# The front of a fused attention and MLP kernel: first batch's q, k loaded in FP32, two blocks' distances added by matmul, second pair ahead of the first layer

## Chip, core and metric

The kernel runs on one core of a Trainium2 chip. The metric is the device time of one launch in microseconds (us); the kernel before has a median of 307.6 us over three runs (307.52 to 308.02). The profile names the engines PE (TensorE), DVE (VectorE), ACT (ScalarE), POOL (GpSimd) and SP (SyncE).

## What is computed

Attention with a sliding window of 128 keys and a linear penalty on distance (ALiBi), for 8 batches, 8 heads, 576 tokens and 64 elements a head; then, on the 512 values of each token, a layer norm with a gain, two weight matrices with a ReLU between them, and a residual.

```python
scores = scale * np.matmul(q, k.transpose(0, 1, 3, 2))
slopes = 2.0 ** (-8.0 * (np.arange(H, dtype=np.float32) + 1) / H)
bias = slopes[:, None, None] * (-np.abs(rel).astype(np.float32))[None, :, :]
mask = (rel >= 0) & (rel < window)
scores = np.where(mask, scores + bias[None], -1000000000.0)
...
attn = np.exp(scores)
attn = attn / (np.sum(attn, axis=-1, keepdims=True) + 1e-09)
return np.matmul(attn, v).astype(np.float32)
...
xn = (x - mu) / np.sqrt(var + 1e-06) * g_ln
ch = np.maximum(xn @ w_ch1, 0.0) @ w_ch2
return (x + ch).astype(np.float32)
```

Inputs and output are FP32 in HBM; the kernel computes in FP16 with FP32 sums.

## The kernel before

**Blocks and groups.** Batches are taken in pairs. A pair has nine blocks of 128 rows: blocks 0 to 7 alternate between the two batches (block 2i is rows 128i of the first batch, block 2i+1 the same rows of the second), block 8 holds the last 64 rows of both. `order` lists the 36 blocks. The MLP takes them in groups: four groups of two blocks, then seven of four (`GROUPS`). Groups 0 and 1 are blocks 0 to 3 of the first pair.

**What one block goes through.** `turn` transposes q and k of two blocks (one of each batch) on PE, 64 matmuls of 64x64 (L317), and copies them out of PSUM (L336, L337). `attend` makes the scores of all heads for keys of the block and of the one before it in the same batch (L430) in one of two PSUM areas `ps_sc`, which alternate, and ACT takes the exponential (L438). Blocks 0 and 1 have one key block and one exponential of 1024 columns; from block 2 on there are two key blocks and two exponentials, heads 0 to 3 ("low") and 4 to 7 ("high"). `masks` multiplies the result on DVE (L449) by a table of the decay `exp(-slope * distance)`, zero outside the window. `values` multiplies by v (L483) in two halves of four heads in a buffer of `ps_mm`; v carries a column of ones, so that the sums come out with it, and DVE divides (L491, L492) and keeps row sums. From block 8 on `values_at_once` does all eight heads in `ps_sc[0]` (L512, L520, L521). `centre` subtracts the mean (L540, and L554 or L563). For blocks 0 to 3 it also multiplies by the gain, from `g_row` (L554), since w1 as loaded has no gain in it; groups from 2 on use `w1g`, made on DVE by `gain_w1` (L193). `turn_x` transposes the centred x on PE (L583) and copies it to `xT` (L584).

**The MLP.** `mlp1(g)` makes the first layer of a group in 16 units of four matmuls (L746); each unit takes a buffer of `ps_mm` (four in all), and its ReLU goes to ACT (L762) or, for the units named in `on_dve`, to DVE (L754). w1 comes in four chunks of four units each. `mlp2` is the second layer (L776); `finish` scales and adds x (L1120).

**Tables.** `distances()` gives five tables of 128x128 in one tensor; `decay(m, at)` makes the decay of all eight heads with ACT exponentials (L149): `m_full` (blocks 0 to 7) and `m_tail` at the start, `m_ends` in the step of block 5's scores.

**Loads.** SP issues the tables (L133, L139), the gain by columns (`g_sb`, L157) and by line (`g_line`, L160). POOL issues all of q, k, v and the weights (L184, L203, L223, L258) and turns FP32 to FP16 on the way. The list `loads` is issued in order: q, k of blocks 0 and 1, v of 0, v of 1, q, k of blocks 2 and 3, v of 2, v of 3, then w1 (four chunks) and half of w2, q, k, v of 4, v of 5, the other half of w2, and so on. `load_until(place[n])` issues up to block n; `values_steps(n)` calls it seven blocks ahead.

**Order of the work.** Inside `tc.manual_schedule` every engine works in the order in which the program text issues. `steps` is a list of small steps of attention; `advance_to(first)` runs those ahead of the first layer, and `weave_at(units, *places)` runs one step after each unit whose number stands in `places`. `warm(n)` issues n matmuls of ones on PE (L299) whose result nobody reads. The first steps are 11 such matmuls, `turn_first` (q and k of blocks 0 and 1, with the gain spread over the partitions by `spread_g` and two more matmuls of ones between), scores and masks of 0 and 1, the values of 0, the turn of blocks 2 and 3, the values of 1, x of 0, scores of 2, x of 1, scores of 3, the first half of block 2's values. The rest of blocks 2 and 3 lies between the units of the first layer.

Of the kernel before, what the change touches and what calls it, by code (L numbers as in the profile page):

```python
# [17 lines left out]
P = 128  # L18
# [45 lines left out]
FAR = 60000.0  # L64


def distances():

    key = np.arange(P)[:, None]
    query = np.arange(P)[None, :]

    def far(rel, ok=True):
        return np.where(ok & (rel >= 0) & (rel < WINDOW), rel, FAR)

    ends = [far(P + query - HALF * b - key, query // HALF == b) for b in range(2)]
    tail = far(query - key, query // HALF == key // HALF)
    evens_first = np.r_[0:P:2, 1:P:2]  # L80
    both = [far(P + query - key), far(query - key)]
    cols = [m[:, evens_first] for m in both] + [*ends, tail]
    return np.concatenate(cols, axis=1).astype(np.float16)
# [3 lines left out]
def kernel(  # L87
# [41 lines left out]

    iden_dram = nc.inline_tensor(np.eye(P, dtype=np.float16), name="iden16")  # L130
    dist_dram = nc.inline_tensor(distances(), name="distances")
    dist = consts.tile([P, 5 * P], FP16)
    nc.sync.dma_start(out=dist, in_=dist_dram.ap())  # L133
    iden = consts.tile([P, P], FP16)
# [4 lines left out]
    nc.sync.dma_start(out=iden, in_=iden_dram.ap())  # L139
# [5 lines left out]
    def decay(m, at):  # L145

        n = m.shape[2]
        for h in range(H):
            nc.scalar.activation(  # L149
                out=m[:, h, :],  # L150
                in_=dist[:, at * P : at * P + n],
                func=AF.Exp,
                scale=-(2.0 ** (-8.0 * (h + 1) / H)),
            )

    g_sb = consts.tile([P, NKB], FP32)
    nc.sync.dma_start(out=g_sb, in_=moe_g_ln.rearrange("(kb p) -> p kb", p=P))  # L157

    g_line = out_pool.tile([P, DM], FP32, tag="o", name="g_line")[0:1]
    nc.sync.dma_start(out=g_line, in_=moe_g_ln.rearrange("(o d) -> o d", o=1))  # L160
    g_row = out_pool.tile([P, DM], FP32, tag="o", name="g_row")
    one_line = consts.tile([1, P], FP32)
# [15 lines left out]
    ht_all = consts.tile([P, NFB, 4 * P], FP16)  # L178
    w1r = moe_w_ch1.rearrange("(kb p) f -> p kb f", p=P)
# [86 lines left out]
    weights = {3: w1s + w2s[:2], 5: w2s[2:]}  # L266
    loads, place = [], []
    for n, (p, blk) in enumerate(order):
        of_v = [(load_v, p, blk)]
        if n >= V_FIRST:  # L270
            loads += of_v
        if blk % 2 == 0:
            for src, tag in ((q, "q"), (k, "k")):
                load = load_natural if by_dma(p, blk) else load_qk
                loads.append((load, src, tag, p, blk // 2))
        if n < V_FIRST:
            loads += of_v
        place.append(len(loads))
        loads += weights.get(n, [])
# [20 lines left out]

    def spread_g():

        ps = ps_mm.tile([P, DM], FP32, tag="mm", name="ps_g")
        nc.tensor.matmul(ps, one_line, g_line, start=True, stop=True)
        return ps
# [65 lines left out]
    def turn_first():  # L371

        q, k = queries(0, 0), keys_tile("k", 0, 0)
        ps = [bank(b)[:, 0] for b in range(2)]
        transposed("q", 0, 0, ps)
        for b in range(2):
            nc.vector.tensor_copy(out=q[:, b], in_=ps[b])
        ps_row = spread_g()
        warm(2)
        ps = [bank(b)[:, 0] for b in (0, None)]  # L380
        transposed("k", 0, 0, ps)
        for b, copy in enumerate((nc.scalar.copy, nc.vector.tensor_copy)):
            copy(out=k[:, b].rearrange("p h (c r) -> p r h c", r=2), in_=ps[b])
        nc.vector.tensor_copy(out=g_row, in_=ps_row)
# [19 lines left out]

    def attend(p, blk, keys, mask, tag, hps, sc=None):
# [15 lines left out]
        ps = banks.rearrange("p j (n t q) -> p j n t q", n=len(hps), t=nk)  # L421
        qt, b = turned["q", p, blk // 2], blk % 2
        for n, hp in enumerate(hps):
            for t, o in enumerate(keys):
                kt = turned["k", p, o // 2][:, o % 2]
                for c, r, queries in seen(p, blk, o, t):
                    cols = slice(c * HALF, (c + 1) * HALF)
                    for j in range(2):
                        rows = slice(j * HALF, (j + 1) * HALF)
                        nc.tensor.matmul(  # L430
                            in_halves(ps[cols, j, n, t, :])[:, r, queries],
                            kt[rows, hp, cols],
                            in_halves(qt[rows, b, hp])[:, r, queries],
                            start=True,
                            stop=True,
                        )
# [7 lines left out]
        unmasked.setdefault((p, blk), []).append((dst, mask[:, heads, :]))  # L444
# [59 lines left out]
    def values_at_once(p, blk):  # L504
# [3 lines left out]
        ps = ps_sc[0].rearrange("p g (h e) -> p (g h) e", h=4)  # L508
# [26 lines left out]
    def centre(p, blk):  # L535
# [3 lines left out]
        if p * NSLOT + blk < BY_DMA:  # L539
# [13 lines left out]
        if p == 0 and blk < FIRST:  # L553
            nc.vector.scalar_tensor_tensor(  # L554
                out=xc,
                in0=xs[p, blk],
                scalar=mean,
                in1=g_row,
                op0=ALU.subtract,
                op1=ALU.mult,  # L560
            )
        else:
            nc.vector.tensor_scalar(  # L563
                out=xc, in0=xs[p, blk], scalar1=mean, scalar2=None, op0=ALU.subtract
            )
# [11 lines left out]
    def turn_x(g, at, p, blk, copy):  # L577
# [6 lines left out]
        copy(out=xT[:, :, at * P : (at + 1) * P], in_=ps)  # L584
# [82 lines left out]


    steps = warm_step(11) + [[(turn_first,)]] + warm_step(3)
    steps += [scores_step(0), scores_step(1) + masks_of(0) + masks_of(1)] + warm_step(6)  # L670
    steps += values_steps(0)
    steps += [turn_step(2, True, (nc.scalar.copy, nc.scalar.copy))]
    steps += values_steps(1) + warm_step(4)
    steps += [x_step(0, nc.scalar.copy)] + warm_step(2) + [scores_step(2)]
    steps += [masks_of(2, 1) + x_step(1) + scores_step(3), values_steps(2)[0]]
    steps += [masks_of(2)]
    first = len(steps)

    steps += [values_steps(2)[1] + masks_of(3)]
    steps += [x_step(2, nc.scalar.copy), *values_steps(3), x_step(3, nc.scalar.copy)]  # L680
# [5 lines left out]
    steps += [values_steps(4)[1], scores_step(5) + [(decay, m_ends, 2)]]  # L686
    steps += [x_step(4) + masks_of(5)]
    steps += [values_steps(5)[0], turn_step(6, True), values_steps(5)[1], scores_step(6)]
    steps += [x_step(5) + masks_of(6), scores_step(7) + variance_of(4), values_steps(6)[0]]
# [44 lines left out]
    hidden = {}  # L734

# [425 lines left out]
    nc.vector.memset(ones, 1.0)  # L1161
    for vx in vext:
        nc.vector.memset(vx[:, :, D : D + 1], 1.0)
    nc.vector.memset(magic, 0x5F3759DF)
    nc.vector.memset(one_line, 1.0)
    decay(m_full, 0)
    decay(m_tail, 4)
    load_until(place[3])
    engine = mybir.EngineType
    with tc.manual_schedule(engines={engine.PE}):  # L1170
        with tc.manual_schedule(engines={engine.Activation, engine.DVE, engine.SP, engine.Pool}):
            advance_to(first)
            weave_at(mlp1(0, (0, 1)), 2, 7, 8, 9, 13)
            weave_at(mlp1(1), 2, 8, 12)
# [59 lines left out]
```

## Time and profile before

| | |
|---|---|
| median of three runs | 307.6 us |
| profiled execution | 307.49 us |
| its span (first to last instruction) | 305.7 us |
| PE busy | 297.9 us (97%) |
| DVE busy | 245.7 us (80%) |
| ACT busy | 182.4 us (60%) |
| POOL busy | 111.7 us (37%) |
| granted TensorE clock | 1.00 throughout |
| first matmul of the first layer (L746) | 19.16 us |
| first matmul of the second layer (L776) | 34.51 us |

An engine is busy while an instruction of its own runs; matmuls are pipelined, so that a busy PE is not yet a PE at its best. Times in the views count from the span's first instruction. The 1.8 us between the span and the execution's time lie outside the profile. A line of a timeline gives start and length, engine, line of the program, operation, what is written and read, the shape, and in brackets the idle time before it and who ended it.

### The profile page before, as it was taken

To read this page: it belongs to the slowest core of one execution; us is meant where nothing else is said; L and a number is where in the kernel's file an instruction comes from. 1 tells how busy PE (TensorE), PEld (TensorE's weight loads), DVE (VectorE), ACT (ScalarE), POOL (GpSimd) and SP (SyncE) were. 2 spreads that over 40 slices of the span, in tenths; PEclk is the share of its full clock that TensorE was granted. 3 is DMA by queue.
4 is the path that set the end of the run, shared out by engine and by line. 5 is a ranking of instruction groups with operands and counts; after the bars stand their busy time and mean duration, and the time that the engine had idled before them with its cause. 6 is when DMAs were issued, how large, how long until landed. Compare 5 with 4: busy or idle time off the path is not lost.

```text
span 305.7 us, 9273 instructions
## 1 busy us (share of the span) xinstructions
PE 297.9 (97%) x3782; PEld 203.6 (67%) x3782; DVE 245.7 (80%) x651; ACT 182.4 (60%) x329; POOL 111.7 (37%) x152
## 2 busy tenths in 40 slices
PE   8889999999999999999999999999999999999994
PEld 2468755856755578646865686568656865698883
DVE  2689878889986899679867986798799878978993
ACT  7588775767966863675368635853586268505500
POOL 8923659673774372475107250760000000000000
PEclk9999999999999999999999999999999999999999
DMA  9999999999999999999999999997661043005014
GB/s 112 172 206 200 189 158 165 196 131 100 138 120 193 145 132 141 182 182 132 131 172 130 114 131 159 121 154 95 97 130 38 19 102 72 19 19 137 3 34 103
DMA packets 150172, 38.03 MB, mean 124 GB/s; under 512 B 140785, under 2 KB 146033, under 8 KB 150130
## 3 DMA queue, kind: packets, MB, share of 16 engines
q0 software_dynamic: 103744, 18.36, 89.0%
q1 hardware_dynamic: 45906, 18.70, 37.7%
q8 instruction: 29, 0.48, 0.7%
q10 hardware_dynamic: 480, 0.39, 0.5%
q14 instruction: 13, 0.11, 0.1%
HBM read 36.90 MB, written 9.44 MB: 152 GB/s over the span
## 4 chain that ended last, share of the span: by engine, by line
PE 90%; DMA 5%; POOL 2%; ACT 2%; issue 1%; DVE 0%; ACTq 0%; POOLq 0%
PE ps_m L746 36%; PE ps_s L976 25%; PE ps_m L776 9%; PE ps_sc L430 6%; PE ps_sc L512 4%; PE ps_q L1055 4%; PE ps_x L870 3%; DMA q<-q 3%; DMA k<-in_k_dram 2%; PE ps_pv L483 1%; POOL q L223 1%; ACT probs L438 1%; PE ps_tr L317 1%; PE ps_sc L317 1%; POOL vx L258 1%
## 5 line engine op out<-in xcount | busy, mean ns | idle before, releaser
L746 PE MATMUL ps_m<-xT,w1g 128*128 128x512 f16 (+1 forms) x512 | 103.8, 353 | 0.0
L762 ACT ACTIVATE ht_all<-ps_m 128x512 f16<-128x512 f32 (+1 forms) x143 | 71.7, 511 | 26.5 <-PE ps_m L746 24.5
L438 ACT ACTIVATE probs<-ps_sc 128x1024 f16<-128x1024 f32 x56 | 56.5, 1029 | 46.4 <-PE ps_sc L430 46.4
L746 PEld LDWEIGHTS <-w1g 128*128 128x128 f16 x512 | 47.6, 98 | 42.6 <-issue 0.4
L258 POOL DMA_DIRECT2D vx<-in_v_dram x40 | 34.0, 859 | 67.1 <-PE ps_sc L512 38.4
L976 PE MATMUL ps_s<-w,s 128*128 128x256 f16 x384 | 43.8, 273 | 0.0
L976 PEld LDWEIGHTS <-s 128*128 128x128 f16 x384 | 36.7, 98 | 4.7
L449 DVE TENSOR_TENSOR probs<-probs,m 128x1024 f16<-128x1024 f16 x56 | 36.9, 684 | 2.5 <-ACT probs L438 2.5
L976 PE MATMUL ps_s<-w,ht_all 128*128 128x256 f16 x288 | 34.3, 273 | 0.0
L776 PE MATMUL ps_m<-w,ht_all 128*128 128x512 f16 x128 | 31.3, 380 | 0.0
L976 PEld LDWEIGHTS <-ht_all 128*128 128x128 f16 x288 | 27.4, 98 | 5.0
L247 POOL DMA_DIRECT2D q<-in_q_dram x40 | 27.4, 698 | 4.9 <-DMA vx<-in_v_dram 2.9
L997 DVE SCALAR_TENSOR_TENSOR o<-ps_s,rstd,x 128x256 f32<-128x256 f32 x48 | 21.0, 478 | 8.4 <-PE ps_s L976 8.4
L796 DVE TENSOR_TENSOR s<-ht_all 128x1024 f16<-128x1024 f16 (+2 forms) x36 | 20.5, 571 | 7.9 <-ACT ht_all L762 6.7
L430 PE MATMUL ps_sc<-q,k 64*64 64x128 f16 (+1 forms) x1088 | 24.1, 209 | 1.1 <-ACT probs L438 0.7
L430 PEld LDWEIGHTS <-k 64*64 64x64 f16 x1088 | 15.8, 106 | 13.1 <-issue 10.9
L594 ACT ACTIVATE junk<-xc 128x512 f16<-128x512 f16 x28 | 17.6, 628 | 5.7 <-DVE xc L563 5.6
L244 POOL DMA_DIRECT2D k<-in_k_dram x20 | 17.9, 910 | 6.8 <-DMA k<-k 5.3
L521 DVE SCALAR_TENSOR_TENSOR x<-ps_sc,rec 128x512 f16<-128x512 f32 x28 | 19.4, 692 | 1.0
L997 DVE SCALAR_TENSOR_TENSOR o<-ps_s,rstd,o 128x256 f32<-128x256 f32 x36 | 15.7, 478 | 3.4 <-PE ps_s L976 3.1
L776 PEld LDWEIGHTS <-ht_all 128*128 128x128 f16 x128 | 11.1, 98 | 10.8
L512 PEld LDWEIGHTS <-probs 128*128 128x128 f16 x352 | 14.6, 98 | 3.5
(109 smaller groups left out, 381.8 us busy)
## 6 DMA issues: line engine op xcount, KB each, us to landing
out_dram<-o SPq DMA_DIRECT2D x64, 128.0 KB, 2.4
k<-in_k_dram POOLq DMA_DIRECT2D x32, 128.0 KB, 6.9
vx<-in_v_dram POOLq DMA_DIRECT2D x32, 128.0 KB, 8.0
w<-in_moe_w_ch_dram POOLq DMA_DIRECT2D x8, 512.0 KB, 10.9
q<-in_q_dram POOLq DMA_DIRECT2D x48, 64.0 KB, 6.3
q<-in_q_dram POOLq DMA_DIRECT2D x12, 128.0 KB, 5.4
out_dram<-o SPq DMA_DIRECT2D x10, 64.0 KB, 1.9
k<-in_k_dram POOLq DMA_DIRECT2D x8, 64.0 KB, 6.7
```

The source lines that it names most:

```text
L247: nc.gpsimd.dma_start(out=t[half, b], in_=tokens.rearrange("h (c r) d -> r c h d", r=2)[r],)
L258: nc.gpsimd.dma_start(out=vx[p0 : p0 + n, :, 0:D], in_=v[b, :, t0 : t0 + n, :].rearrange("h p d -> p h d"),)
L430: nc.tensor.matmul(in_halves(ps[cols, j, n, t, :])[:, r, queries], kt[rows, hp, cols], in_halves(qt[rows, b, hp])[:, r, queries], start=Tr ...
L438: nc.scalar.activation(out=dst.rearrange("p (n j) q -> p j n q", j=2), in_=ps.rearrange("p j n t q -> p j n (t q)"), func=AF.Exp, scale=in ...
L449: nc.vector.tensor_tensor(out=dst, in0=dst, in1=mask, op=ALU.mult)
L512: nc.tensor.matmul(ps[:, h, 0 : D + 1], pr[:, h, t, :], vext[(p * NSLOT + o) % NV][:, h, :], start=(n == 0), stop=(n == len(terms) - 1),)
L746: nc.tensor.matmul(ps[:, 0:cols], w[:, kb, fb * P : (fb + 1) * P], xT[:, kb, 0:cols], start=(kb == 0), stop=(kb == NKB - 1),)
L762: nc.scalar.activation(out=ht[:, fb, :], in_=ps[:, 0:cols], func=AF.Relu)
L776: nc.tensor.matmul(sums[at], ht[:, fb, at * P : (at + 1) * P], w2[:, fb, :], start=(fb == 0), stop=(fb == NFB - 1),)
L796: nc.vector.tensor_tensor(out=out, in0=a, in1=b, op=op)
L976: nc.tensor.matmul(ps[:, pair, :], lhs[:, fb, at : at + P], rhs[:, fb, :], start=(first and pair == 0 and fb == 0), stop=(fb == half - 1), ...
L997: nc.vector.scalar_tensor_tensor(out=outs[at][:, cols], in0=ps[:, pair], scalar=rstd[:, n : n + 1], in1=(xs[p, blk] if fresh else outs[at] ...
```

## The change

- **Loads.** q and k of the first batch's block 0 come in FP32, k issued by ACT and q by SP behind the tables, into the first part of `ht_all` (which the first layer writes later), q in partitions 0 to 63, k in 64 to 127. `cast_first` turns them to FP16, four heads on DVE, four on ACT. q and k of the second batch's block 1 come by POOL as before (`load_first`). `start()` issues all loads up to block 7 at once. w1's first chunk moves ahead of v of block 2; the second half of w2 ahead of v of block 5.
- **Tables.** The identity and the two tables of `m_full` come in one load (`first_tables`, 96 KB), the others later by POOL, behind v of block 5 (`more_tables`). `m_tail` is made at x of block 5. `m_full` is made in two halves, the second behind the exponentials of blocks 0 and 1.
- **Distances by matmul.** For blocks 0 and 1 (`ADDED`), `slopes` makes slope times distance on DVE, `add_distances` puts it in PSUM with the identity as the weights, and the scores add onto it; no mask follows. `FAR` is 16000, so that the products fit FP16.
- **Gain.** `g_row`, `spread_g` and the load of `g_sb` go. `g_columns` makes `g_sb` from `g_line` with four matmuls; the gain of groups 0 and 1 is applied as `turn_x` copies out of PSUM, on DVE in one multiply or on ACT in four scaled copies of 128 columns.
- **Order.** The second pair is turned, with one batch's copies on DVE and the other's on ACT, and block 2 scored ahead of the first layer; block 3's scores and both blocks' values follow between its units. Values of blocks 0 to 3 are made at once, in either area of `ps_sc`. The filler matmuls go from 28 to 14. `mlp1_pair` takes the units of groups 0 and 1 in the order 12, 8, 4, 8.

```diff
-    weights = {3: w1s + w2s[:2], 5: w2s[2:]}
+    weights = {3: w1s[1:] + w2s[:2], 4: w2s[2:], 5: [(load_tables,)]}
...
-        if blk % 2 == 0:
+        if n == 0:
+            loads += [(load_first, nc.gpsimd, first_qk[1], src, 1) for src in (q, k)]
+        elif blk % 2 == 0:
...
+        if n == 2:
+            loads += w1s[:1]
...
+    def load_first(queue, to, src, b):
+        rows = slice(0, HALF) if src is q else slice(HALF, P)
+        queue.dma_start(
+            out=to[rows],
+            in_=src[b, :, 0:P, :].rearrange("h (c r) d -> c h r d", r=2),
+        )
+
+    def cast_first():
+        for copy, heads in ((nc.vector.tensor_copy, slice(0, 4)), (nc.scalar.copy, slice(4, H))):
+            copy(out=first_qk[0][:, heads], in_=first_fp32[:, heads])
...
+    def slopes():
+
+        for h in range(H):
+            nc.vector.tensor_scalar(
+                out=bias[:, h],
+                in0=first_tables[:, 2 * P :],
+                scalar1=-(2.0 ** (-8.0 * (h + 1) / H)) / inv_sqrt_d,
+                scalar2=None,
+                op0=ALU.mult,
+            )
...
+    def turn_first(b, copy):
+
+        if b == 0:
+            first_turned.extend((queries(0, 0), keys_tile("k", 0, 0)))
+        q, k = first_turned
+        ps = [bank()[:, 0] for _ in range(2)]
...
+        nc.vector.tensor_copy(out=q[:, b], in_=ps[0])
+        copy(out=k[:, b].rearrange("p h (c r) -> p r h c", r=2), in_=ps[1])
...
+    def add_distances(banks):
+
+        for j in range(2):
+            nc.tensor.matmul(
+                banks[:, j].rearrange("p (n c) -> p n c", n=HP),
+                iden,
+                bias.rearrange("p (n j) c -> p j n c", j=2)[:, j],
+                start=True,
+                stop=False,
+                skip_group_check=True,
+            )
...
-                            start=True,
+                            start=not added,
...
-        copy(out=xT[:, :, at * P : (at + 1) * P], in_=ps)
+        dst = xT[:, :, at * P : (at + 1) * P]
+        if g >= FIRST_GROUPS:
+            copy(out=dst, in_=ps)
+            return
+
+        if copy == nc.vector.tensor_copy:
+            nc.vector.tensor_tensor(
+                out=dst, in0=ps, in1=g_sb.unsqueeze(2).broadcast_to([P, NKB, P]), op=ALU.mult
+            )
+            return
+        for kb in range(NKB):
+            nc.scalar.activation(
+                out=dst[:, kb], in_=ps[:, kb], func=AF.Copy, scale=g_sb[:, kb : kb + 1]
+            )
...
-    steps = warm_step(11) + [[(turn_first,)]] + warm_step(3)
-    steps += [scores_step(0), scores_step(1) + masks_of(0) + masks_of(1)] + warm_step(6)
-    steps += values_steps(0)
-    steps += [turn_step(2, True, (nc.scalar.copy, nc.scalar.copy))]
-    steps += values_steps(1) + warm_step(4)
-    steps += [x_step(0, nc.scalar.copy)] + warm_step(2) + [scores_step(2)]
-    steps += [masks_of(2, 1) + x_step(1) + scores_step(3), values_steps(2)[0]]
-    steps += [masks_of(2)]
+    (low2, high2), (low3, high3) = ([[(attend, *args)] for args in attends(*order[n])] for n in (2, 3))
+    steps = warm_step(6) + [[(slopes,), (decay, m_full, range(4))]]
+    steps += [[(add_distances, ps_sc[b]) for b in range(2)], [(cast_first,)]]
+    steps += [[(turn_first, 0, nc.scalar.copy)], [(turn_first, 1, nc.vector.tensor_copy)]]
+    steps += [[(g_columns,)]] + warm_step(2)
+    steps += [scores_step(0), scores_step(1), [(decay, m_full, range(4, H))]] + warm_step(3)
+    steps += [[(values_at_once, 0, 0, 0), (centre, 0, 0)]] + warm_step(3)
+    steps += [[(values_at_once, 0, 1, 1)], x_step(0, nc.scalar.copy), [(centre, 0, 1)]]
+    steps += [turn_step(2), x_step(1), low2, high2]
     first = len(steps)
 
-    steps += [values_steps(2)[1] + masks_of(3)]
-    steps += [x_step(2, nc.scalar.copy), *values_steps(3), x_step(3, nc.scalar.copy)]
+    steps += [masks_of(2, 1) + low3, masks_of(2) + high3]
+    steps += [masks_of(3, 1) + [(values_at_once, 0, 2, 0)], masks_of(3) + [(centre, 0, 2)]]
+    steps += [[(load_until, place[10]), (values_at_once, 0, 3, 1), (centre, 0, 3)]]
+    steps += [x_step(2, nc.scalar.copy), x_step(3)]
...
-            weave_at(mlp1(0, (0, 1)), 2, 7, 8, 9, 13)
-            weave_at(mlp1(1), 2, 8, 12)
+            weave_at(mlp1_pair((0, 12), (0, 8), (12, NFB), (8, NFB)), 1, 1, 1, 3, 5, 6, 9, 18, 24, 28)
```

## The prediction

> **What bounds the kernel now.** I read the page's shares first: TensorE (PE) is busy for 297.9 of 305.7 us, so time can be had only where PE is idle, slow or fed with filler. The view by windows shows where that is.
>
> ```profile
> core 0: us, PE busy (x) PEld busy (x) DVE busy (x) ACT busy (x) POOL busy (x), PEclk, DMA share, GB/s
> 0.00:19.13 19.13, 15.51 (x286) 7.46 (x287) 9.94 (x38) 13.33 (x28) 15.81 (x25) 1.00 1.45 155
> 19.13:34.65 15.52, 15.49 (x168) 13.73 (x165) 14.22 (x49) 13.19 (x33) 5.88 (x8) 1.00 1.49 195
> 34.65:54.40 19.75, 19.75 (x371) 10.62 (x369) 15.45 (x42) 12.44 (x22) 13.57 (x21) 1.00 1.63 169
> ```
>
> From 19.13 us, where the first layer of groups 0 and 1 begins, PE has no gap worth naming. The 15.51 us before it are mostly filler (28 matmuls of ones). So a change of the front is worth what it moves the start of the first layer, less the work and the waits that it puts behind that start. The chain of waits, followed to the front, says what sets the start:
>
> ```profile
> 1.24 1.50 POOL q L223 x2
> 2.74 1.36 POOL k L223 x2
> 4.10 1.76 POOL vx L258 x2
> 5.86 0.71 POOL q L223 x2
> ...
> 7.81 5.57 DMA k<-in_k_dram
> ...
> 13.92 0.56 ACT q L336
> 14.49 0.63 ACT k L337
> 15.12 0.45 ACT q L336
> 15.57 0.64 ACT k L337
> 16.21 0.45 ACT xT L584
> 16.66 1.85 ACT probs L438 x2
> ```
>
> POOL's issues in order, the landing of the second pair's k at 13.4, then ScalarE (ACT) alone: four copies, xT, two exponentials. The timeline has the rates and the first exponentials:
>
> ```profile
> 1.46 4.88 PE L299 MATMUL ps_warm<-ones 128*128 128x512 f16 x11 [1.46 <-DVE vx L1163]
> 9.97 1.94 ACT L438 ACTIVATE own<-ps_sc 128x1024 f16<-128x1024 f32 x2 [0.52 <-PE ps_sc L430]
> 10.07 1.47 PE L299 MATMUL ps_warm<-ones 128*128 128x512 f16 x6
> 26.65 8.02 PE L746 MATMUL ps_m<-xT,w 128*128 128x256 f16 x72
> ```
>
> A warm matmul takes 0.44 us at first (4.88/11) and 0.25 later (1.47/6); a first-layer unit (four matmuls) takes 0.44 (8.02/18).
>
> **The front, step by step (starting times in us).** Landings come from the trace, issue by issue. POOL's q and k of pair 0: issued at 1.24, 2.04, 2.71, 3.43, landed 3.8 to 3.9 later (5.1, 5.9, 6.5, 7.2). Second pair's k: issued 7.9, landed 13.4. v of blocks 2, 3: 14.4, 15.3. w1 chunk 0 at 17.5, chunk 2 at 22.6, chunk 3 at 25.2, one per 2.55.
>
> 1. *FP32 q, k of batch 0.* SP and ACT issue them at about 0.75 to 1.2. No row has an FP32 load of 512 pieces on those queues. Bounds: 2.3 to landing (the 160 KB table) and 5.8 (k behind a full queue). The nearest row is the same pattern on POOL's queue, 3.8: landed at about 5.0. Casts: 128x512 on DVE between 0.35 and 0.69 (rows of xc), ACT's copy 0.6: done at 5.7. The k issue holds ACT some 0.4 before its first exponentials, covered by the table's landing (ACT waited 1.03 for it).
> 2. *Slopes and distances.* Eight DVE multiplies of 128x128, between 0.07 (the vx memsets) and 0.41 (L193, four times the columns): I take 0.15, 1.2 in all, 2.95 to 4.2. Four matmuls of 512 columns, 0.25 to 0.44, taken slow: PE to 5.9. They cover the landing of step 1 and replace both masks of blocks 0, 1 (2 x 0.69 on DVE, the first on the path).
> 3. *Batch 1 on POOL.* q, k issued at 1.24 and 2.0: 5.9 if as now, 7.8 with k's later 5.8. 512 KB of FP32 now share the transfers: the old front had read 1.2 MB by 7.2, the new one needs 1.1; I take 6.6. Transposes 0.45, DVE copies 0.42 and 0.73: k ready 8.2. g_columns: four small FP32 matmuls, 0.2 to 0.6 each (rows of 64 columns and of L304), and one copy of 0.2; then warm 2.
> 4. Scores of block 0 follow at 8.2, its exponential at 8.75 (now 9.97), the next at 9.75. Values, without a mask: 10.2. DVE from there: reciprocal and product 1.0, centring 0.55, twice, 10.6 to 13.6 (one row at 0.69 instead of two halves at 0.43; centring by 0.35 in place of 0.75). The other half of m_full (1.3 on ACT) lies beside it.
> 5. *Second pair.* q and k are issued 1.2 earlier, but fewer bytes precede them by 94 KB only: landed about 12.4. Copies now one batch on DVE (1.15, 13.6 to 14.75) beside the other on ACT, instead of 2.3 on ACT. x of block 1 with g on DVE, 0.42 to 0.75: 15.4. ACT's four scaled copies of block 0: 4 x 0.21 to 0.29 (spacing and row of m_tail), beside DVE.
> 6. w1 chunk 0 goes ahead of v of blocks 2, 3 (0.95 of transfer each): landed 14.8, not binding. **First layer at 15.5, 3.65 earlier.** Lower bound 14.8 (batch 1 at 5.9); upper 16.9 (k at 7.8, slow slopes).
>
> **What goes behind that start.** Scores of block 3 (0.57 in the chain) and half the values of block 2 (0.24): +0.8. After unit 1 stand three steps in one place. ACT's exponentials of blocks 2 and 3 run 15.1 to 19.1, 0.96 each, back to back. PE after unit 1 (16.4) does low3, waits 0.4 for the bank of high2 and some 0.65 for that of low3, as values 2 use the same bank; values of block 3 wait about 0.3 for the mask on DVE, whose queue holds two relus, the masks and block 2's product. Queued behind each wait are the units themselves. Less the 0.35 of gaps that this stretch has now: +1.0. Weights: chunk 1 at 19.1, chunk 2 at 21.6 (1 earlier than now), needed at 19.4 and 21.9; chunk 3 only after 20 units. w2's second half goes ahead of v of block 5, some 1.9 earlier, for a need 1.8 earlier.
>
> ACT has 3.9 of exponentials, 30 relus at 0.43 and about 1.0 of x copy: 17.7 in a stretch of 17.3 on PE. With four PSUM buffers it may lag by three units, so this costs nothing yet. Without that cover each us more on ACT would cost PE about one.
>
> m_tail's eight exponentials (1.69) move to ACT at about 51.5, in the 1.56 that ACT idles before block 7's scores: at most 0.15. The later tables leave POOL behind v of block 5, landing near 40 by the 8.4 of that time's q; m_ends wants them at 42. POOL's later loads stay in order and shift along; SP's transposes too, whose q at 85.8 lands just as PE comes, so a few tenths may be lost there.
>
> **Sum:** -3.65 + 0.8 + 1.0 + 0.15 = -1.7. Against the profiled execution's own 307.49 (1.8 outside the span) that is 305.8; the median of the runs, 307.6, gives 305.9. I say **305.8**. The case's own range is 304.7 to 306.9 (start 14.8 to 16.4, the rest as above).
>
> **A rule against the change.** The Trainium skill, DMA: Bandwidth & Descriptors, section Issuing engines are not separate DMA queues, says that loads started by different engines end up on the same transfer engines, and that a second issuer saves only its issue time. The trace is on its side for the time after 4 us (mean share over 1.7 in several windows of 1 us, landings growing from 3.8 to 5.8), against it before: 0.17 and 0.64 in the windows 1 to 2 and 2 to 3. By the rule alone the result is rival 2.
>
> **Rivals.**
> 1. *Fewer waits.* If landings come as early as step 1's lower bound and batch 1 at 5.9, the start is 14.8, and if the bank waits (1.0) vanish too: -2.4 - 1.0 from the sum's other end: 304.2. For it: w1 is there at 14.8. Against it: the four exponentials are one ACT chain whatever the start.
> 2. *The transfers are the bound.* FP32 traffic delays batch 1's k to 7.8 or the second pair's k to its old 13.4: start 16.6, -2.55 + 1.95 = -0.6: 306.9. For it: service already lags POOL's issue by 2 us at 9. Against it: idle transfer time before 3 us.
> 3. *The slow rate comes back* (the side of slower). Filler falls from 28 matmuls to 14. PE needed from 1.46 to about 5.7 of solid matmuls to pass from 0.44 to 0.25; if the thinner front doesn't bring that, the distances, transposes and scores cost some 0.5 more and the first layer runs its first 4.3 us at half rate, 2.15: -1.7 + 2.65 = +0.95: 308.4. It decides from the point where PE is idle for most of a stretch of that length before 15.5. For it: gaps while batch 1 lands. Against it: now, from 11 to 19, PE is idle 2.6 of 8 us and the rate holds. The Trainium skill, TensorE: Matmul & The Clock Gate, Part 1, gives such a rule: idle windows of about 3.4 us bring half rate back; the page's granted clock of 1.00 doesn't show the slow start that the durations do.
> 4. *ACT becomes the bound in the weave* (its backlog above four buffers, with exponentials 1.5 later): each late relu holds a unit, +1.7: 307.5, no change. For it: 17.7 against 17.3.
>
> Chances: forecast 0.50, rival 1 0.16, rival 2 0.12, rival 3 0.12, rival 4 0.10. A measurement here tells 0.2% (0.6 us) from no change. Forecast, rival 1 and half of rival 2 (0.06) are faster: 0.72, less 0.02 for the forecast's weak end (half to each of the others): 0.70. Same: half of rival 4, the rest of rival 2: 0.12. Slower: rival 3 and half of rival 4: 0.18. The range, 303.9 to 308.0, leaves out rival 3 and the ends.
>
> **What would show it.** The first L746 matmul's start (15.5), the first own exponential (8.75) not followed by a mask, batch 0's casts near 5 to 6, PE's idle time after unit 1 put down to probs, and the end of the 32 units (32.9 against 34.65). The prediction is wrong if the units start after 17, if they take 0.87 us each at first, or if PE waits for w1 or in the mlp2 stage.

## The result, and the profile after

The changed kernel takes 310.59 us in the median of its runs against 307.81 for the kernel before on the same chips: a ratio of 1.0082 (95% interval 1.0059 to 1.0106). I had forecast 305.8, a gain. Its profiled execution took 1668.66 us with every matmul at about a sixth of its rate (1.31 us for a matmul of ones of 512 columns), so the profile of a later run of the same kernel, `r1_after`, is read here: span 308.0 us, 2.3 above the 305.7 of before.

The view by windows of `r1_after`, divided where its first layer starts and ends (the columns are busy us and instructions of each engine, the granted clock, the transfers):

```profile
core 0: us, PE busy (x) PEld busy (x) DVE busy (x) ACT busy (x) POOL busy (x), PEclk, DMA share, GB/s
0.00:19.00 19.00, 14.06 (x242) 7.91 (x243) 8.36 (x39) 9.62 (x20) 14.49 (x23) 0.82 1.55 169
19.00:36.56 17.56, 16.70 (x201) 14.56 (x202) 15.24 (x47) 15.37 (x37) 7.39 (x10) 1.00 1.41 199
36.56:56.81 20.25, 19.92 (x370) 10.78 (x369) 14.31 (x40) 13.98 (x29) 14.38 (x20) 1.00 1.89 155
```

The first layer starts at 19.00, where it started before (19.16), and not at 15.5. What lies behind the start came out as costed: 17.56 us for the 32 units and the work among them (forecast 17.4, before 15.5). So the front won nothing and the work put behind it was paid: 36.56 against 34.65 at the end of that stretch. The rest of the 2.3 is 0.4: the next stage takes 20.25 us against 19.75, and what follows 0.1 less. And the clock column reads 0.82 in the front, where it read 1.00 before.

The chain of waits of `r1_after` shows the front in order of time (start, length, what):

```profile
1.17 5.80 DMA ht_all<-in_q_dram
...
7.08 0.44 DVE first L204
...
7.56 0.55 PE ps_tr L437 x32
8.11 0.42 DVE q L442
...
8.57 1.86 PE ps_g L210 x8
10.44 0.97 PE ps_warm L357 x2
11.40 1.00 PE ps_sc L502 x31
12.40 1.39 PE ps_warm L357 x3
13.79 0.46 PE ps_sc L586 x8
```

The reader sees two things. The FP32 load of q is the first link, 5.80 us, landing at 7.0. And between 8.6 and 13.8 the chain is PE alone, with matmuls of ones at 0.46 to 0.49 (1.39/3, 0.97/2) and the four one-column products of the gain (eight matmuls in the trace) at 1.86 in all. A finer view by windows of the same kernel shows the rate:

```profile
core 0: us, PE busy (x) PEld busy (x) DVE busy (x) ACT busy (x) POOL busy (x), PEclk, DMA share, GB/s
4.00:6.00 2.00, 1.51 (x5) 0.40 (x3) 0.00 (x0) 0.11 (x1) 2.00 (x4) 1.00 1.46 199
6.00:8.00 2.00, 0.44 (x48) 0.44 (x52) 0.43 (x1) 0.62 (x1) 1.98 (x3) 1.00 2.90 153
8.00:10.00 2.00, 1.76 (x47) 1.65 (x32) 1.39 (x3) 0.73 (x1) 1.77 (x3) 0.58 2.34 160
10.00:12.00 2.00, 2.00 (x33) 1.15 (x36) 0.16 (x1) 0.00 (x0) 2.00 (x4) 0.50 1.62 193
12.00:14.00 2.00, 2.00 (x27) 1.01 (x20) 0.00 (x0) 1.97 (x3) 1.72 (x3) 0.50 1.35 198
14.00:16.00 2.00, 1.74 (x18) 0.86 (x16) 1.53 (x6) 1.18 (x4) 0.44 (x1) 0.71 2.11 173
```

PE is busy for 0.44 us between 6 and 8, and after that it runs at half rate: the missing shares (0.42, 0.50, 0.50, 0.29 of 2 us each) are 3.42 us, or 6.84 us at half. That is rival 3, in the front and not in the first layer.

### The profile page after: what moved, and what is told of

It is laid out like the page before. It is cut to its first block, busy times and chain, and to the rows that moved or that the text cites. A ratio compares the mean times of both kernels' runs of the same rounds, so it can differ in the third digit from the quotient of the medians.

```text
span 1666.9 us, 9271 instructions
## 1 busy us (share of the span) xinstructions
PE 1661.4 (100%) x3778; PEld 694.7 (42%) x3778; DVE 250.0 (15%) x649; ACT 189.5 (11%) x333; POOL 110.9 (7%) x151
## 3 DMA queue, kind: packets, MB, share of 16 engines
q0 software_dynamic: 102736, 18.20, 14.4%
## 4 chain that ended last, share of the span: by engine, by line
PE 100%; DVE 0%; issue 0%
PE ps_m L839 41%; PE ps_s L1069 27%; PE ps_m L869 10%; PE ps_sc L586 5%; PE ps_q L1148 4%; PE ps_sc L502 4%; PE ps_x L963 3%; PE ps_warm L357 1%; PE ps_tx L647 1%; PE ps_tr L369 1%; PE ps_pv L557 1%; PE ps_s L963 1%; PE ps_t L963 1%; PE ps_sc L369 0%; PE ps_sc L467 0%; PE ps_g L210 0%
## 5 line engine op out<-in xcount | busy, mean ns | idle before, releaser
L839 PE MATMUL ps_m<-xT,w1g 128*128 128x512 f16 (+1 forms) x512 | 597.5, 1521 | 0.0
L839 PEld LDWEIGHTS <-w1g 128*128 128x128 f16 x512 | 151.3, 301 | 378.0 <-issue 377.7
L1069 PE MATMUL ps_s<-w,s 128*128 128x256 f16 x384 | 254.1, 1036 | 0.0
L1069 PE MATMUL ps_s<-w,ht_all 128*128 128x256 f16 x288 | 193.0, 1033 | 0.0
L869 PE MATMUL ps_m<-w,ht_all 128*128 128x512 f16 x128 | 173.0, 1667 | 0.0
L1069 PEld LDWEIGHTS <-s 128*128 128x128 f16 x384 | 119.0, 313 | 123.6 <-issue 123.3
L1069 PEld LDWEIGHTS <-ht_all 128*128 128x128 f16 x288 | 87.8, 308 | 100.4 <-issue 100.0
L586 PEld LDWEIGHTS <-probs 128*128 128x128 f16 x384 | 73.8, 247 | 34.7 <-issue 34.7
L839 PE MATMUL ps_m<-xT,w 128*128 128x256 f16 x128 | 85.9, 1044 | 0.0
L586 PE MATMUL ps_sc<-vx,probs 128*128 128x65 f16 x384 | 79.5, 477 | 0.0
L869 PEld LDWEIGHTS <-ht_all 128*128 128x128 f16 x128 | 34.3, 278 | 88.9 <-issue 88.5
```

Source lines behind the costliest of these rows:

```text
L586: nc.tensor.matmul(ps[:, h, 0 : D + 1], pr[:, h, t, :], vext[(p * NSLOT + o) % NV][:, h, :], start=(n == 0), stop=(n == len(terms) - 1),)
L839: nc.tensor.matmul(ps[:, 0:cols], w[:, kb, fb * P : (fb + 1) * P], xT[:, kb, 0:cols], start=(kb == 0), stop=(kb == NKB - 1),)
L869: nc.tensor.matmul(sums[at], ht[:, fb, at * P : (at + 1) * P], w2[:, fb, :], start=(fb == 0), stop=(fb == NFB - 1),)
L1069: nc.tensor.matmul(ps[:, pair, :], lhs[:, fb, at : at + P], rhs[:, fb, :], start=(first and pair == 0 and fb == 0), stop=(fb == half - 1), ...
```

## The experiments

Two theories were set against each other. A: the slow rate came back because PE idled while it waited for the first q and k. B: the FP32 loads land late, the transfers are the bound, and the rate is a side effect.

### The same kernel again

> The changed kernel once more, nothing edited, for a profile of an ordinary execution: the one on record ran 1668.66 us with every matmul at about a sixth of its rate, while five unprofiled runs of the same kernel took 309.67 to 310.86 at a mean granted clock of 0.988 to 0.998 (before: 1.000). Theory A (the slow rate comes back in the front): about 310.5 us, a granted clock near 0.99, and one stretch of some 7 us between 5 and 30 us in which it is near half and a unit of the first layer takes 0.87 us instead of 0.44. Theory B (the transfers are the bound): the same time, but the granted clock dips only where PE idles, units at 0.44 throughout, and PE's waits put down to DMA of k, q or w. In both the first FP32 load of q lands near 7 us, not 5.

309.0 us, granted clock 0.994, in a single execution. One stretch at half, 9.9 to 13.4 us, ahead of the first layer, whose units took 0.44 us throughout; first layer at 17.92. q landed at 7.0. So neither expectation fits whole: the rate did come back, but for 3.4 us and not 7, and no unit of the first layer ran at half. The stretch at half differs between executions of one kernel (3.4 us here, 6.8 in `r1_after`). That it makes the whole difference of their times is not shown: two other executions took 310.53 us at a mean granted clock of 0.998 and 309.67 at 0.992.

> Control: the changed kernel, unedited, beside the three edits of this set. 309.0 to 311; a granted clock below 1.000 (0.988 to 0.994) from one or two stretches of some 3.5 us at half rate between 9 and 18 us; the first FP32 load of q landed near 7.0.

309.8 us, ratio to the kernel before 1.0067 (1.0043 to 1.0092). This is the control, with which the next three are compared.

### Filling the gap

```diff
-    steps += [[(add_distances, ps_sc[b]) for b in range(2)], [(cast_first,)]]
+    steps += [[(add_distances, ps_sc[b]) for b in range(2)]] + warm_step(4) + [[(cast_first,)]]
```

> Four more matmuls of ones behind the distances, where PE idles from 6.0 to 7.5 for the casts of the first batch. Theory A (the slow rate came back because PE idled there): the granted clock is 1.000, matmuls of ones take 0.25 us each behind 8 us and the time is 1.8 to 3.4 us below the control, near 307. Theory B (the landing of the FP32 q decides, the rate is a side effect): the casts still start at 7.0, the first own exponential comes no more than 0.6 us earlier than the control's 10.8 and the time falls by under 0.7 us.

307.93 us, ratio 1.0011 (0.9985 to 1.0037), 1.9 below the control. The timeline of `e1_fill` (start, length, engine, line, what, shape, idle time before):

```profile
6.90 0.62 ACT L204 CAST first<-ht_all 128x512 f16<-128x512 f32 x1 [2.78 <-DMA ht_all<-in_q_dram]
7.53 0.74 PE L437 MATMUL ps_tr<-first_tables,first 64*64 64x64 f16 x64 [1.45 <-DVE first L204]
8.51 1.05 PE L210 MATMUL ps_g<-one,g_line 1*128 1x1 f32 x8 [0.23 <-DVE q L442]
10.49 1.94 ACT L511 ACTIVATE own<-ps_sc 128x1024 f16<-128x1024 f32 x2 [1.69 <-PE ps_sc L502]
17.09 1.03 PE L839 MATMUL ps_m<-xT,w 128*128 128x256 f16 x8
```

The casts start when they did (6.90 against 7.06), but the gain's products take 1.05 instead of 1.86, the first exponential starts at 10.49 instead of 12.03, and the first layer at 17.09 instead of 19.00: 1.91 earlier, all of the time won. That useless work ahead of the casts keeps the rate, and is worth 1.9 us, is shown. The single executions bear it out: eight of the ten executions of `e1_fill` took 307.66 to 308.74 us at a granted clock of 0.997 to 1.000, and the two that lost the rate (0.992 and 0.993) took 309.86 and 310.17, like the control. With six such matmuls (`e4_g_late`, `e8_values` below) all 24 executions show 0.997 or more. That PE's idle time is what decides, as theory A has it, is not shown. In this profile PE still idles for 1.45 us ahead of the transposes, against 1.57 in `e0_after` and 2.05 in `r1_after`. Theory B isn't refuted by it either, since q still lands 2 us later than I had costed.

### The loads

```diff
-            loads += [(load_first, nc.gpsimd, first_qk[1], src, 1) for src in (q, k)]
+            loads += [(load_first, nc.gpsimd, first_qk[b], src, b) for b in range(2) for src in (q, k)]
...
-    steps += [[(add_distances, ps_sc[b]) for b in range(2)], [(cast_first,)]]
+    steps += [[(add_distances, ps_sc[b]) for b in range(2)]]
...
-        load_first(nc.scalar, first_fp32, k, 0)
-        load_first(nc.sync, first_fp32, q, 0)
```

> The FP32 loads undone alone: q, k of both first batches by POOL in FP16, in the order q0, k0, q1, k1; no casts; the rest of the change stays. Theory B: the four land at 5.1, 5.9, 6.5 and 7.2 as in the kernel before, PE turns the first batch at 6.0 and the second at 7.4, the first own exponential starts near 9.4 instead of 10.8, w1's first chunk lands no later, and the time is 1.2 to 2 us below the control. Theory A alone: PE still has a gap before 7.4 and half its old filler, so the clock dips as in the control and less than 0.7 us is won.

309.99 us, 1.0064 (1.0038 to 1.0090): the control's time. POOL's loads did land early, the first batch was turned at 5.70 instead of 7.56, but PE then waited 0.9 and 0.8 for the second batch, the rate was at half from 8.9 to 15.7, and the first layer started at 18.73. Here the earlier landing brought nothing, as the rate went; theory B's own forecast failed.

> POOL first clears 128x4096 elements of w1g (written over later), so that its loads start some us later; a look at the landing of the FP32 k and q, not at the time, which must grow. If the FP32 loads are late because they share the transfers with POOL's: k and q land 2.5 to 4 us after their issues (3.3 to 5.2 us) with POOL still silent. If 512 pieces of 512 bytes on SP's and ACT's queues are slow in themselves: 3.9 and 5.8 us after issue as in the changed kernel, q near 7.0.

POOL's first load was issued at 4.22 instead of 1.24, in one execution. The landing view of the FP32 staging tile (k and q; least, median, most), first of `e3_late_pool`:

```profile
DMA to landing us min/median/max: 4.0/4.3/4.6
```

and of `r1_after`:

```profile
DMA to landing us min/median/max: 3.8/4.8/5.8
```

k takes 3.8 to 4.0 either way. q takes 4.6 without POOL's traffic beside it and 5.8 with it. Of the 2.0 us by which q was late against my 3.8, 1.2 go with POOL's traffic. The other 0.8 stay without it; that they come from k's load, issued 0.44 us earlier, is likely but was not tried alone. Neither expectation fits by itself. The run's time, 311.13, holds one more thing, told in the last section.

### What stood on PE's path

`e4_g_late` holds the rate with six matmuls of ones and moves the gain's products behind the scores:

```diff
-    steps += [[(g_columns,)]] + warm_step(2)
-    steps += [scores_step(0), scores_step(1), [(decay, m_full, range(4, H))]] + warm_step(3)
+    steps += warm_step(2)
+    steps += [scores_step(0), scores_step(1), [(g_columns,), (decay, m_full, range(4, H))]] + warm_step(3)
```

> The changed kernel with six matmuls of ones before the casts (so that the rate holds), and the four matmuls and the copy of the gain's columns moved from ahead of block 0's scores to behind block 1's; two matmuls of ones stay ahead of the scores. Theory: with the rate held, g_columns (1.05 us in that place in e1_fill) is the next thing on the path; block 0's scores then wait for k's copy only: first own exponential near 9.4 instead of 10.5, first layer near 16.0 instead of 17.1, time 0.9 to 1.2 us below e1_fill's 307.9, near 306.9, a ratio to the kernel before of about 0.997. Rival (the second pair's landing near 12 and DVE's chain of values and copies decide): the exponential comes earlier, the first layer does not, and the time stays within 0.3 of e1_fill.

307.87 us, 1.0007 (0.9991 to 1.0023). The exponential came at 9.49, as expected, the first layer only at 16.61, and the time stayed at `e1_fill`'s, as the rival had it. The reason was another than the rival's: in the timeline the gain's products and three matmuls of ones now stood ahead of block 0's values (11.46), whose weights were ready at 10.5. `e8_values` puts the values first:

```diff
-    steps += [scores_step(0), scores_step(1), [(g_columns,), (decay, m_full, range(4, H))]] + warm_step(3)
-    steps += [[(values_at_once, 0, 0, 0), (centre, 0, 0)]] + warm_step(3)
+    steps += [scores_step(0), scores_step(1), [(decay, m_full, range(4, H))]] + warm_step(2)
+    steps += [[(values_at_once, 0, 0, 0), (centre, 0, 0)], [(g_columns,)]] + warm_step(2)
...
-    steps += [turn_step(2), x_step(1), low2, high2]
+    steps += [turn_step(2)] + warm_step(2) + [x_step(1), low2, high2]
```

> e4_g_late with the values of block 0 ahead of the gain's columns, and filler moved: two matmuls of ones behind block 1's scores, two behind the columns, two behind the second pair's turn (20 in all, as there). In e4_g_late the first own exponential came 1.0 us earlier than in e1_fill but the first layer only 0.48, because on PE the columns (1.05) and three matmuls of ones stood ahead of block 0's values (11.46, their exponential done at 10.5). Theory: values at 10.5, DVE's chain and the first layer 0.9 earlier (15.7), time 0.6 to 0.9 us below e4_g_late: a ratio to the kernel before of 0.997 or 0.998. Rival (the second pair's landing near 12 or w1's first chunk near 15.1 decides): first layer at 16.3 or later, ratio 1.000 or above.

307.04 us, ratio 0.9965 (0.9938 to 0.9991): a small gain over the kernel before, and clearly faster than the changed kernel. Its timeline:

```profile
9.55 1.94 ACT L511 ACTIVATE own<-ps_sc 128x1024 f16<-128x1024 f32 x2 [0.70 <-PE ps_sc L502]
10.63 0.43 PE L586 MATMUL ps_sc<-vx,own 128*128 128x65 f16 x8
10.99 1.05 PE L210 MATMUL ps_g<-one,g_line 1*128 1x1 f32 x8
16.04 1.03 PE L839 MATMUL ps_m<-xT,w 128*128 128x256 f16 x8
```

Values at 10.63, first layer at 16.04 (expected 15.7): 3.1 earlier than the kernel before, of which the work behind the start takes 2.1 (17.66 us against 15.52 for the 32 units).

### The waits among the units

```diff
-            weave_at(mlp1_pair((0, 12), (0, 8), (12, NFB), (8, NFB)), 1, 1, 1, 3, 5, 6, 9, 18, 24, 28)
+            weave_at(mlp1_pair((0, 12), (0, 8), (12, NFB), (8, NFB)), 1, 2, 4, 5, 7, 8, 11, 18, 24, 28)
```

> e4_g_late with the three steps behind unit 1 spread over units 1, 2 and 4 and the two behind them over 5 and 7 (x of blocks 2, 3 behind 8 and 11). Theory (PE's waits for the exponentials behind unit 1, 0.36 and 0.50 in every trace of the changed kernel, are lost time): both waits go, the 32 units and what lies between them take 16.6 instead of 17.5 us, time 0.7 to 0.9 us below e4_g_late. Rival (ACT is the bound of this stretch, 17.7 us of work): the waits come back as units held for a PSUM buffer, and less than 0.3 us is won.

308.47 us, 1.0027 (1.0007 to 1.0047), 0.6 above `e4_g_late`. Both waits went, but the first unit of group 1 waited 0.8 for x of block 3. The places 1, 2, 4, 5, 6, 7, 10 on top of `e8_values` were meant to mend that:

> e8_values with the three steps behind unit 1 spread over units 1, 2 and 4, the next over 5, 6 and 7 and x of block 3 behind unit 10 (in e5_spread it stood behind 11, and the first unit of group 1 waited 0.8 for it). Theory: the two waits for exponentials (0.36, 0.50) go and the wait for xT falls to 0.3, so 0.4 to 0.6 us less than e8_values. Rival (ACT and DVE are the bound here): no better than e8_values.

308.19 us, 1.0005 (0.9984 to 1.0027), 1.15 above `e8_values`. The timeline of `e9_spread`:

```profile
19.05 1.06 ACT L511 ACTIVATE probs<-ps_sc 128x1024 f16<-128x1024 f32 x1
19.35 0.61 PE L839 MATMUL ps_m<-xT,w 128*128 128x256 f16 x4 [0.32 <-DMA w<-in_moe_w_ch_dram]
22.09 0.42 PE L586 MATMUL ps_sc<-vx,probs 128*128 128x65 f16 x8 [0.53 <-DVE mean L623]
25.62 1.59 PE L839 MATMUL ps_m<-xT,w 128*128 128x256 f16 x13 [0.30 <-DVE xT L654]
```

The unit that PE does while it would have waited puts its ReLU on ACT ahead of the last exponential, which now ends at 20.1 instead of 19.7 in `e8_values`; the steps placed after later units add to it, block 3's last mask on DVE starts at 21.35 instead of 20.34, and block 3's values and x follow. The 32 units take 18.3 us instead of 17.66. So the rival's forecast holds, and in this order the chain through ACT and DVE sets most of the time. One more wait was new: the fifth unit came early enough to wait 0.32 us for w1's second chunk, on which `e8_values` shows no wait.

### Two parts undone

> e5_spread with the FP32 loads undone: all four first loads by POOL in FP16 (q0, k0, q1, k1), no casts, block 0 scored ahead of the second batch's turn, eight matmuls of ones around them. Theory (FP32 loads on SP and ACT cost more than they bring, since they land at 4.7 and 7.0 while POOL's first two land at 5.1 and 5.9): first own exponential near 7.5, the second near 9.8; the first layer then waits for the second pair and w1's first chunk, which are issued 1.3 later: start between 15.3 and 16.3, time within 0.7 of e5_spread, and below it if the theory of DVE's chain holds. If the FP32 loads bring what they were costed to bring, it is 0.7 us or more above e5_spread.

The base is `e5_spread`; the edit is that of `e2_pool`, with block 0 scored ahead of the second batch's turn. 310.0 us, 1.0066 (1.0038 to 1.0095). The first exponential came at 7.85, the first layer at 16.70 (16.90 in `e5_spread`): without FP32 loads the start is as early. The view by windows of `e6_pool`:

```profile
core 0: us, PE busy (x) PEld busy (x) DVE busy (x) ACT busy (x) POOL busy (x), PEclk, DMA share, GB/s
12.00:14.00 2.00, 1.22 (x27) 0.75 (x29) 1.86 (x7) 0.40 (x3) 2.00 (x4) 1.00 1.27 190
14.00:16.00 2.00, 1.23 (x76) 0.88 (x76) 1.93 (x7) 2.00 (x6) 0.82 (x2) 1.00 2.04 167
16.00:18.00 2.00, 2.00 (x35) 1.44 (x36) 0.69 (x2) 1.86 (x3) 1.08 (x2) 0.54 1.44 200
18.00:20.00 2.00, 2.00 (x35) 1.08 (x37) 1.57 (x4) 1.11 (x2) 0.98 (x2) 0.61 1.24 207
```

In this profile the half rate falls on the first layer itself, as rival 3 had it: (0.46 + 0.39) x 2 us = 1.7 lost. Too little work on PE ahead of it does not explain that alone, since PE is busy for 2.45 of the 4 us from 12 to 16 here and for the same 2.45 in `e4_g_late`, which kept the rate. Nor does the stretch explain the run's time: the other six executions took 308.55 to 311.73 us at granted clocks of 0.997 to 1.000. So the price of the loads by themselves stays open.

The traces do show one regularity. Every stretch at half in a front lasts 3.41 us or twice that, so the rate changes in steps of 3.41. In the 3.41 us ahead of each loss PE was busy for 1.36 us (`r1_after`), 2.17 (`e0_after`), 1.72 (`e2_pool`) and 1.86 (`e6_pool`). `e4_g_late` has such a stretch too, 12.54 to 15.95 with 1.86, and kept the rate. So busy time in such a stretch does not sort them by itself. It may be that the work is counted within fixed steps that the kernel does not place, or that small matmuls count for less; neither was tested.

```diff
-ADDED = 2
+ADDED = 0
...
-    steps = warm_step(6) + [[(slopes,), (decay, m_full, range(4))]]
+    steps = warm_step(6) + [[(decay, m_full, range(H))]]
-    steps += [[(add_distances, ps_sc[b]) for b in range(2)]] + warm_step(6) + [[(cast_first,)]]
+    steps += warm_step(10) + [[(cast_first,)]]
...
-    steps += [scores_step(0), scores_step(1), [(g_columns,), (decay, m_full, range(4, H))]] + warm_step(3)
+    steps += [scores_step(0), scores_step(1) + masks_of(0) + masks_of(1), [(g_columns,)]] + warm_step(3)
```

> e5_spread with the distances by matmul undone: blocks 0 and 1 get their masks on DVE again, no slopes, no added distances (ten matmuls of ones ahead of the casts instead of six). Theory: each mask is 0.69 us in DVE's chain ahead of the first layer, so the first layer starts 0.7 to 1.4 us later and the time grows as much over e5_spread. Rival (DVE has slack there, the second pair's landing decides): within 0.3 us.

309.07 us, 1.0040 (1.0018 to 1.0062) against `e5_spread`'s 1.0027. The first layer starts at 16.84 against 16.90: with the masks back on DVE it is no later, since in this order PE brings the values late anyway. The medians differ by 0.6 us, the intervals overlap, and the traces show no loss in the front, so a gain from the added distances is not shown.

### A stall inside block 5's scores

All profiles of the changed kernel and its variants up to here stand for 0.2 to 1.0 us inside the scores of block 5 with nothing to wait for. The timeline of `r1_after`:

```profile
43.14 0.64 PE L502 MATMUL ps_sc<-q,k 64*64 64x128 f16 x30
44.11 0.24 PE L502 MATMUL ps_sc<-q,k 64*64 64x128 f16 x2 [0.33 <-issue]
```

and of `e1_fill`, with four more matmuls on PE in the front:

```profile
41.24 0.58 PE L502 MATMUL ps_sc<-q,k 64*64 64x128 f16 x26
42.10 0.30 PE L502 MATMUL ps_sc<-q,k 64*64 64x128 f16 x6 [0.28 <-issue]
```

The place moved from behind matmul 30 to behind 26 of these scores; counted from the start it is behind PE's 606th matmul in both. `e10_cut` is `e8_values` with twelve matmuls of ones cut into four each (`nc.tensor.matmul(ps[:, cols], ones[:, 0:P], ones[:, cols])`, 128 columns), which is 36 more instruction pairs:

> e8_values with twelve of its matmuls of ones cut into four of 128 columns each: the same columns, 36 more instruction pairs on PE ahead of the first layer. In seven profiles PE stood 0.2 to 1.0 us inside block 5's scores, behind matmul 30 (the changed kernel), 26 (four matmuls more), 25 (five more) and 24 (six more): always the same place in PE's instruction stream. Theory (PE waits there for its next piece of instructions): the place moves 36 pairs up, to the second-layer matmuls ahead of block 5's scores, there is no stall inside these scores any more, and it is shorter or gone where each matmul lasts 0.22 us; the time falls by 0.2 to 0.6 us. Rival (the stall belongs to the scores, their PSUM bank or their data): it stays behind matmul 24.

Its timeline at the same scores, whole:

```profile
41.02 0.64 PE L503 MATMUL ps_sc<-q,k 64*64 64x128 f16 x32
```

The stall is gone from there, but it did not move 36 pairs up as expected, and the 606th matmul has none. Another of 0.8 stands in the second pair's transposes at 13.9, behind the 223rd, where `e8_values` had none. 307.44 us, 0.9984 (0.9961 to 1.0008), so the forecast gain over `e8_values` did not come. That the stall does not belong to the scores or their data is shown; it went with the position in PE's instruction stream wherever only a few matmuls were added. That PE waits there for its next piece of instructions (the profile's page lists 29 pieces of them, 0.48 MB, on a queue of their own) fits, but was not measured by itself.

## Why the prediction was wrong

It forecast 305.8 in 303.9 to 308.0 with the sign of a gain; the kernel is 2.8 us slower. By its own steps:

- **Step 1, the FP32 loads: wrong value.** I took the 3.8 us of POOL's first loads as the nearest row and 5.8 as the far bound. k took 3.8, q took 5.8. I had counted the bytes, and that the transfers idle before 3 us, but the bytes of four loads fall due together from 3 to 7 us. This made the casts start at 7.06 instead of 5.1 and PE's transposes at 7.56 instead of 5.9: 1.66 us. The rule of the Trainium skill that I quoted against the change (DMA: Bandwidth & Descriptors, Issuing engines are not separate DMA queues) has loads from several engines share the transfer engines. The trace agrees: 1.2 of q's 5.8. The second batch on POOL was late too: its q and k landed 5.4 and 5.7 after their issue, k at 7.7, where step 3 took 6.6 and rival 2 had 7.8.
- **Step 2: right.** The eight multiplies took 1.2 us, the four added products ran to 5.5 to 6. But I called them cover for step 1, and the cover was too short by 1.5 to 2 us. That gap is the trigger of the next point.
- **Rival 3, given 0.12, is what happened, and took 1.9 of the 3.5 us.** I had the trigger (filler cut from 28 to 14, a gap while the first batch lands) and wrote against it that the kernel before bears 2.6 idle us in 8 (the view has 2.1: busy 5.91 of 8 from 11 to 19). But those come in pieces of at most half a microsecond; here 2 us were empty in one piece, with only 64x64 transposes behind. The price was 1.9 us and not 2.65, and in the changed kernel it was paid ahead of the first layer, so that no unit took 0.87. The Trainium skill (TensorE: Matmul & The Clock Gate, Part 1) has the rate follow windows of about 3.4 us, and half rate come after an idle one. The lengths agree: the stretches at half were 3.4, 6.8 and 3.4 us in `e0_after`, `r1_after` and `e6_pool`. An idle window was not needed: PE was busy for 1.36 to 2.17 of the 3.41 us ahead of each loss.
- **Step 3, g_columns: left off the path.** Its matmuls were costed at 0.2 to 0.6 each, but the scores of block 0 were let follow k's copies at 8.2 as if the products and the two matmuls of ones fitted beside the copies. They took 1.05 at full rate and 1.86 at half, and the matmuls of ones 0.6 to 1.0, on PE ahead of the first scores: these started at 10.02 in `e1_fill` and 9.02 in `e4_g_late`, where the products stand behind them.
- **Steps 4 to 6: right in size.** From the first exponential to the first layer I had 6.75; it took 6.97 in `r1_after` and 6.60 in `e1_fill`.
- **Behind the start: right.** 17.56 against 17.4, with the two waits at 0.36 and 0.50 (costed 0.4 and 0.65). ACT did not become the bound in that order (rival 4), as the waits stayed what they were; `e9_spread` shows how near it is.
- **Missed:** 0.2 to 1.0 us of the stall in block 5's scores, which no row of before shows. w1 and w2 were never waited for in the changed kernel, as forecast.

The account of the span: forecast -1.7; 3.5 later at the first layer (1.9 of it the half rate, 1.6 the landing and the products), 0.15 more among the units, some 0.3 in block 5's scores: +2.25 by the terms, and 2.3 measured. The terms are read from the same trace as the span, so their sum is no further proof. Of the 1.6, about 1.05 went when the products were moved (first layer at 16.04 in `e8_values` against 17.09); the other 0.5 was not taken apart.

The idea of the change was sound. With the rate held and the values of block 0 ahead of the gain's products the same kernel takes 0.9965 (0.9938 to 0.9991) of the time before; about half of the gain that I had forecast for it as it stood. It is one measurement: the same order with its filler in smaller pieces, `e10_cut`, has 0.9984 with an interval that reaches past 1.

## What to carry to other kernels

Filler matmuls in a front are not always slack: before any are cut, or work is moved so that PE waits in one piece, add up PE's busy time over each 3.4 us. Here stretches with 1.4 to 2.2 us of work lost the rate in some cases and kept it in others, so stay well above that and run the kernel many times, because the half rate is paid by all PE work in the 3.4 or 6.8 us that follow. When several loads are issued at once to be early, cost the last of them by the busy row, not by the first row of an idle queue. On an engine that works in order, put small products that are needed late (here a gain's columns) behind whatever feeds the longest chain, and leave a short wait alone if filling it delays the engine that the chain runs through.

## What the hardware showed that I had not expected

**The clock column reads 1.00 until a first change is recorded.** In `e3_late_pool` the page's mean granted clock is 1.000 and the windows read 1.00 from the start. Its timeline says otherwise:

```profile
10.75 1.03 PE L357 MATMUL ps_warm<-ones 128*128 128x512 f16 x2
```

Two matmuls of ones take 1.03, as at half rate; in `e8_values` the same two take 0.59 to 0.61. There the front stayed at the slow rate until 14.4 us at least (three matmuls of ones in 1.47 us from 14.43), and the column does not tell; how much of its 311.13 us this makes, beside POOL's late loads, was not separated. For the same reason a granted clock near 1.000 does not prove a fast front. The rate in a front is to be read from the durations of a known matmul, not from that column.

**Small multiplies on DVE took twice as long while POOL cleared memory.** The eight multiplies of 128x128 took 0.18 to 0.62 us each in `r1_after` and up to 1.63 in `e3_late_pool`, where POOL was clearing memory; the group took 2.36 instead of 1.20. This is one execution; nothing else was tried.
